# 1110 further matmuls behind the last instruction of TensorE in a fused attention and MLP kernel

## The chip, the cores and the metric

The kernel runs on one core of a Trainium2 chip. The metric is the device time of one execution in microseconds (us). Each engine of the core takes its own instructions in order: TensorE (PE, whose weight loads the profile lists apart as PEld), VectorE (DVE), ScalarE (ACT), GpSimd (POOL) and SyncE (SP, which here only issues DMAs). They meet in semaphores. The program is over when all of them have met in a barrier behind their last instruction.

## The reference

Attention over a window of 32 positions plus 32 global positions for 8 batches and 8 heads, and then an MLP with a GELU over the rows that it gives. Cut to what is computed:

```python
s_g = scale * np.matmul(q_g, k_all.transpose(0, 1, 3, 2))
out_g = np.matmul(sm(s_g), v_all)
mask = np.abs(pos[:, None] - pos[None, :]) <= window
s_ll = np.where(mask, scale * np.matmul(q_l, k_l.transpose(0, 1, 3, 2)), -1000000000.0)
s_l = np.concatenate([scale * np.matmul(q_l, k_g.transpose(0, 1, 3, 2)), s_ll], axis=-1)
out_l = np.matmul(sm(s_l), np.concatenate([v_g, v_l], axis=2))
...
h = x @ w_in                                          # 4352 x 512 by 512 x 2048
g = 0.5 * h * (1.0 + erf(h * inv_sqrt2))
return (g @ w_out).astype(np.float32)                 # 4352 x 2048 by 2048 x 512
```

## The kernel before

The 4352 rows are worked in 17 chunks of 256: sixteen of a batch and a half of its sequence, and one, called "g", of the global rows. For each chunk the attention of four pairs of heads yields x, and then the MLP runs over 16 slices f of 128 of the 2048 columns. For a slice, `ml_hc` makes h by products with four blocks of 128 rows of `w_in` (twelve matmuls of 256 columns), and `ml_o` adds to the two accumulators acc0 and acc1 (six matmuls of 512 columns). Every operand is split into a high and a low part of type float32r (x into `xh` and `xl`, GELU's output into `gh` and `gl`, the weights into `wh` and `wl`), and a product is taken as three: high by high, low by high and high by low. That is why the matmuls come in threes, lines 711 to 713 for h and 746 to 748 for acc:

```python
nc.tensor.matmul(out=h, lhsT=hi, rhs=xh, start=..., stop=False, skip_group_check=True)
nc.tensor.matmul(out=h, lhsT=hi, rhs=xl, start=False, stop=False, skip_group_check=True)
nc.tensor.matmul(out=h, lhsT=lo, rhs=xh, start=False, stop=..., skip_group_check=True)
```

Here `lhsT` is the stationary operand, 128 by 128, which a weight load brings into the array ahead of each matmul, and `rhs` is the moving one, whose 256 or 512 columns stream through. For h the weights are stationary and x moves; for acc the columns of g are stationary and the weights move.

A planner at the end of `attn_mlp` (a list of steps with needs, durations and due times) fixes the order, and the loop `for t, i, x in order` writes the steps out. It ties each instruction to the one before it on the same engine, through the table `last`, so that each engine's order is the planned one.

After the first chunks all 32 tiles of weights stay in SBUF to the end: `wh[n]` in halves of tiles of 1024 columns and `wl_[n]` in tiles of 512. PSUM holds eight banks of 512 columns; two of them, of the pool `ps_h` with the tag "h", take h in turn.

At the end of the program there is only the MLP of the chunk "g": TensorE alternates between twelve matmuls for h and six for acc, ScalarE and GpSimd prepare `gh` and `gl` beside it, and then `ml_e` copies the accumulators out (tile `ob`, line 134) and `ml_w` writes them to DRAM (line 761).

Of the kernel before, what the change touches and what calls it, by code (L numbers as in the profile page):

```python
# [8 lines left out]
F32 = mybir.dt.float32  # L9
# [75 lines left out]
def attn_mlp(ctx, tc, q_l, k_l, v_l, q_g, k_g, v_g, w_in, w_out, out):  # L85
# [1002 lines left out]
    for t, i, x in order:  # L1088
# [14 lines left out]
            taker[kind] = ins[seen].name, ins[seen].engine  # L1103
        seen = len(ins)


# [1 line left out]
_INS = ['q_l', 'k_l', 'v_l', 'q_g', 'k_g', 'v_g', 'moe_w_in', 'moe_w_out']  # L1108
# [26 lines left out]
```

## Time and profile before

| | us |
|---|---|
| median of 2 runs | 1043.26 |
| lowest, highest | 1042.47, 1044.06 |
| the profiled execution | 1045.66 |
| its span, first to last instruction | 1043.8 |
| TensorE busy in it | 1006.6 (96%) |
| granted TensorE clock, mean | 0.998 of full speed |

A row of the timeline has the start in us from the span's start, the duration, engine, line, operation and the tiles, written one first. Durations of matmuls overlap, because they are pipelined: how long one takes on TensorE is the distance from its start to that of the next, called its step below. Rounded to 0.01 us in the rows, it is read over many of them.

### The profile page before, as it was taken

The page shows a single profiled execution, that of the slowest core. Times are in us where ns is not written, and L with a number is a line of the kernel's source. Part 1 is how long each engine was busy: PE and PEld are TensorE (multiplying, and loading weights), DVE is VectorE, ACT ScalarE, POOL GpSimd, SP SyncE. Part 2 cuts the span into 40 slices and gives each one's busy share as a digit, 9 for nine tenths or more (in the row PEclk, how much of TensorE's full clock was granted, in tenths as well). Part 3 has the DMA queues.
Part 4 walks back from the last instruction along what each step waited for, and adds up shares of the span by engine and source line. Part 5 has one row for each costly group of instructions (what it writes and reads, how often), then busy time and mean ns, then how long its engine had stood idle before and what let it go on. Part 6 is the DMA issues. An engine that isn't in the chain of part 4 may idle for free.

```text
span 1043.8 us, 21420 instructions
## 1 busy us (share of the span) xinstructions
PE 1006.6 (96%) x7000; PEld 894.8 (86%) x7000; DVE 684.9 (66%) x2089; ACT 677.0 (65%) x1617; POOL 379.7 (36%) x427
## 2 busy tenths in 40 slices
PE   3889999999998999999999999999999999999998
PEld 2666689989888989898999989998999989999997
DVE  2878978667676877777775777677776777572000
ACT  2868887667567866677675766677575766674232
POOL 2111576243332533343442524334343525233121
PEclk9999999999999999999999999999999999999999
DMA  6877232223221233223322232313322332101000
GB/s 165 239 207 260 51 72 54 49 45 77 57 59 36 38 77 66 63 39 60 79 43 55 55 82 53 65 31 61 82 39 57 62 71 58 48 14 56 1 21 21
DMA packets 277983, 72.29 MB, mean 69 GB/s; under 512 B 263152, under 2 KB 271344, under 8 KB 277872
## 3 DMA queue, kind: packets, MB, share of 16 engines
q1 hardware_dynamic: 271792, 68.57, 28.7%
q10 hardware_dynamic: 6080, 2.36, 0.9%
q8 instruction: 55, 0.90, 0.4%
q14 instruction: 56, 0.46, 0.1%
HBM read 61.41 MB, written 9.44 MB: 68 GB/s over the span
## 4 chain that ended last, share of the span: by engine, by line
PE 75%; ACT 7%; SPq 6%; DMA 5%; DVE 4%; issue 2%; POOL 1%; ACTq 0%; DVEq 0%; POOLq 0%
PE h L711 10%; PE acc L746 9%; PE h L712 9%; PE h L713 9%; PE acc L748 9%; PE acc L747 9%; PE o L519 5%; PE s L408 4%; PE acc L738 2%; PE t L482 2%; ACT a_t L281 2%; PE h L707 2%; PE go L652 2%; ACT L281 1%; DMA raws<-in_q_l_dram 1%
## 5 line engine op out<-in xcount | busy, mean ns | idle before, releaser
L141 POOL TENSOR_TENSOR gl<-gf,gh 128x512 fp32r<-128x512 f32 x127 | 167.8, 1321 | 400.4 <-ACT gh L134 280.1
L711 PE MATMUL h<-xh,wh 128*128 128x256 f32 x1024 | 296.6, 290 | 1.4 <-ACT gf L281 1.4
L712 PE MATMUL h<-xl,wh 128*128 128x256 f32 x1024 | 286.1, 279 | 0.0
L713 PE MATMUL h<-xh,wl 128*128 128x256 f32 x1024 | 285.6, 279 | 0.0
L746 PE MATMUL acc<-wh,gh 128*128 128x512 f32 x512 | 204.9, 400 | 0.0
L711 PEld LDWEIGHTS h<-xh,wh 128*128 128x128 f32 x1024 | 192.7, 188 | 10.2 <-ACT gf L281 1.8
L748 PE MATMUL acc<-wl,gh 128*128 128x512 f32 x512 | 200.4, 391 | 0.0
L747 PE MATMUL acc<-wh,gl 128*128 128x512 f32 x512 | 200.2, 391 | 0.0
L712 PEld LDWEIGHTS h<-xl,wh 128*128 128x128 f32 x1024 | 193.0, 188 | 5.7 <-issue 0.7
L713 PEld LDWEIGHTS h<-xh,wl 128*128 128x128 f32 x1024 | 193.9, 189 | 0.0
L281 ACT ACTIVATE gf<-h 128x512 f32<-128x512 f32 x136 | 81.2, 598 | 69.4 <-POOL gl L141 34.9
L281 ACT ACTIVATE a_t<-a_t,sm 128x192 f32<-128x192 f32 (+1 forms) x256 | 116.8, 458 | 1.9 <-DVE sm L433 1.1
L748 PEld LDWEIGHTS acc<-wl,gh 128*128 128x128 f32 x512 | 96.1, 188 | 21.1
L427 DVE CUSTOM_DVE_ANT_0 a_t<-s,mask 128x192 f32<-128x192 f32 (+1 forms) x256 | 80.4, 368 | 44.0 <-PE s L408 43.8
L134 ACT ACTIVATE gh<-gf 128x512 fp32r<-128x512 f32 x95 | 60.0, 632 | 75.7 <-PE acc L748 74.7
L746 PEld LDWEIGHTS acc<-wh,gh 128*128 128x128 f32 x512 | 96.3, 188 | 12.2
L747 PEld LDWEIGHTS acc<-wh,gl 128*128 128x128 f32 x512 | 96.4, 188 | 11.2
L134 ACT ACTIVATE at<-t 128x512 fp32r<-128x512 f32 (+1 forms) x112 | 59.5, 542 | 48.2 <-PE t L483 21.2
L502 DVE TENSOR_TENSOR at<-t,at 128x512 fp32r<-128x512 f32 (+1 forms) x112 | 67.5, 617 | 34.6 <-ACT at L134 33.9
L141 POOL TENSOR_TENSOR vs<-vr,vs 128x512 fp32r<-128x512 f32 x56 | 74.6, 1332 | 41.8 <-DVE vs L136 19.9
L281 ACT ACT_TABLE_LOAD x69 | 88.5, 1283 | 1.2
L550 DVE TENSOR_TENSOR xs<-o,xs 64x256 f32<-64x256 f32 x112 | 46.1, 412 | 49.0 <-ACT xs L545 47.9
(132 smaller groups left out, 1736.1 us busy)
## 6 DMA issues: line engine op xcount, KB each, us to landing
wraw<-in_moe_w_out_dram SPq DMA_DIRECT2D x16, 512.0 KB, 7.8
raws<-in_v_l_dram SPq DMA_DIRECT2D x64, 128.0 KB, 2.5
out_dram<-ob SPq DMA_DIRECT2D x32, 256.0 KB, 2.2
raws<-in_k_l_dram SPq DMA_DIRECT2D x224, 36.0 KB, 1.9
vr<-in_v_l_dram SPq DMA_DIRECT2D x113, 64.0 KB, 2.1
wraw<-in_moe_w_in_dram SPq DMA_DIRECT2D x14, 512.0 KB, 7.6
raws<-in_q_l_dram SPq DMA_DIRECT2D x224, 32.0 KB, 1.8
raws<-in_v_g_dram SPq DMA_DIRECT2D x128, 16.0 KB, 1.9
```

The lines of the kernel that those rows point to most:

```text
L134: nc.scalar.activation(out=out, in_=in_, func=AF.Copy)
L141: (nc.vector if e == "v" else nc.gpsimd).tensor_sub(**kw)
L281: nc.scalar.activation(func=func, **kw)
L427: nc.vector.tensor_tensor_reduce(out=a_t[:, j, aoff[half][i]:aoff[half][i] + w], in0=s[:, c:c + w], in1=masks[half][i], scale=1.0, scalar= ...
L502: nc.vector.tensor_sub(out=at[:, 1], in0=st.pop((u, "t", j))[:, :n * P].rearrange("p (n q) -> p n q", q=P), in1=at.bitcast(F32)[:, 0])
L519: nc.tensor.matmul(out=o[:, :, qsl], lhsT=l.rearrange("p s e -> p (s e)"), rhs=r, start=(n == 0), stop=(n == 3), skip_group_check=True)
L711: nc.tensor.matmul(out=h, lhsT=hi, rhs=xh, start=(c == 0 and not (key == (0, 0) and f < HQ and f % 2)), stop=False, skip_group_check=True)
L712: nc.tensor.matmul(out=h, lhsT=hi, rhs=xl, start=False, stop=False, skip_group_check=True)
L713: nc.tensor.matmul(out=h, lhsT=lo, rhs=xh, start=False, stop=(c == NCC - 1), skip_group_check=True)
L746: nc.tensor.matmul(out=acc[t], lhsT=gh[:, f % 2, tsl], rhs=hi, start=(f == 0), stop=False)
L747: nc.tensor.matmul(out=acc[t], lhsT=gl[:, f % 2, tsl], rhs=hi, start=False, stop=False)
L748: nc.tensor.matmul(out=acc[t], lhsT=gh[:, f % 2, tsl], rhs=lo, start=False, stop=(f == NF - 1))
```

## The change

Behind the loop that writes out the plan, 1110 matmuls are appended whose results nothing reads. They read weights that lie in SBUF and write to the two banks of the tag "h". No step of the plan is changed, and no other engine gets an instruction.

- `mo()` stands for one acc step: six matmuls of 512 columns, three into each of two banks.
- `h(w, x)` stands for one h step: twelve matmuls of 256 columns into one bank, with the stationary operand from column w and the moving one from column x of their tiles.
- `both(w, x)` is twice a `mo()` and an `h(w, x)`, so 36 matmuls; it is called 28 times: 8 times with w = 0, 8 times with w = 64 and 12 times with other w. That is 336 matmuls of 512 columns and 672 of 256.
- The short runs repeat one matmul: six runs of ten with 256 columns, then four and three runs of six with 512 columns, so 60 and 42.

Together these are 378 of 512 columns and 732 of 256. In bytes, the places are these. Before, and with d = 0 in the new code, the moving operand of an h starts 192 bytes behind the stationary one, modulo 256; with d = 4, 8 or 12 columns it starts 208, 224 or 240 behind, and no longer at a multiple of 64. That holds for 348 of the 732 (288 in `h` and the 60 in runs). The moving and stationary operands of `mo` differ by 0 modulo 256, as they do in an acc before. In the runs of 512 columns 36 of 42 have the stationary operand at no multiple of 64 bytes.

```diff
+    def after_all(e0):
+        ins = nc.cur_bb.bb.instructions
+        for y in ins[e0:]:
+            if y.engine in last:
+                behind(y, last[y.engine])
+            last[y.engine] = y.name
+
+    code = iter([a + b for a in "abcdefghijkmnpqrstuvwxyz" for b in "abcdefghijkmnpqrstuvwxyz"])
+
+    def bank(n):
+        return n, ps_h.tile([P, 512], F32, name="z" + next(code), tag="h")
+
+    def mm(t, st_, mv):
+        n = mv.shape[-1]
+        nc.tensor.matmul(out=t[:, 0:n], lhsT=st_, rhs=mv, start=True, stop=True, skip_group_check=True)
+
+    e0 = len(nc.cur_bb.bb.instructions)
+    H = [wh[n] for n in range(2 * NF)]
+    LO = [wl_[n] for n in range(2 * NF)]
...
+    T1, T2, T3, T4, T5, T6 = H[2], H[6], H[10], H[14], LO[1], LO[9]
+
+    def run(a, b, n=8, w=256, A=None, B=None):
+        _, t = bank(0)
+        for _ in range(n):
+            mm(t, T5[:, b:b + P], T1[:, a:a + w])
+
+    def mo(lo=0):
+        t = [bank(0)[1] for _ in range(2)]
+        for i in range(2):
+            for m, g in ((T1, 64), (T1, 192), (T2, 64)):
+                mm(t[i], T5[:, g + 128 * i:g + 128 * i + P], m[:, 0:512])
+
+    def h(w, x):
+        _, t = bank(0)
+        for c in range(4):
+            for m, g in ((T3, T4), (T6, T4), (T3, LO[17])):
+                mm(t, g[:, w:w + P], m[:, x:x + 256])
+
+    def both(w, x):
+        for _ in range(2):
+            mo()
+            h(w, x)
+
+    for a in (48, 112):
+        for d in (0, 4, 8, 12):
+            both(0, a + d)
+    for a in (48, 112):
+        for d in (0, 4, 8, 12):
+            both(64, (a + d + 64) % 128)
+    for w in (16, 32, 48, 80, 96, 112):
+        for a in (48, 112):
+            both(w, (a + w) % 128)
+    for d in (4, 8, 12):
+        for a in (48, 112):
+            run(a + d, 0, 10)
+    for d in (0, 4, 8, 12):
+        run(0, 64 + d, 6, 512)
+    for d in (4, 8, 12):
+        run(0, d, 6, 512)
+    after_all(e0)
```

TensorE's last instructions before, in order, with the accumulators as `acc_13651` and `acc_13652`; "waits" names the engine whose semaphore a row waits for:

```order
L746 MATMUL acc_13651<-wh,gh 128x512 [waits Activation_49]
L747 MATMUL acc_13651<-wh,gl 128x512 [waits DVE_49]
L748 MATMUL acc_13651<-wl,gh 128x512
L746 MATMUL acc_13651<-wh,gh 128x512
L747 MATMUL acc_13651<-wh,gl 128x512
L748 MATMUL acc_13651<-wl,gh 128x512
L746 MATMUL acc_13652<-wh,gh 128x512
L747 MATMUL acc_13652<-wh,gl 128x512
L748 MATMUL acc_13652<-wl,gh 128x512
L746 MATMUL acc_13652<-wh,gh 128x512
L747 MATMUL acc_13652<-wh,gl 128x512
L748 MATMUL acc_13652<-wl,gh 128x512
L1130 UNCONDITIONAL_BRANCH
```

The branch ends TensorE's part. In the changed program it comes 1110 matmuls later; this is a stretch in the middle of them on the same engine, where zay and zba and zbb are banks of a `mo()` and zaz is that of an `h()`:

```order
L1120 MATMUL zay<-wh,wl 128x512 [waits PE_49]
L1120 MATMUL zay<-wh,wl 128x512 x2
L1120 MATMUL zaz<-wh 128x256 [waits PE_49]
L1120 MATMUL zaz<-wl,wh 128x256
L1120 MATMUL zaz<-wh,wl 128x256
...
L1120 MATMUL zba<-wh,wl 128x512 [waits PE_49]
L1120 MATMUL zba<-wh,wl 128x512 x2
L1120 MATMUL zbb<-wh,wl 128x512 [waits PE_49]
L1120 MATMUL zbb<-wh,wl 128x512 x2
```

What is new beside the matmuls is that each group's first row waits for TensorE's own semaphore: for the end of the group before the last, which wrote the same bank.

More of the change, by code (lines that the diff above doesn't have):

```diff
@@ L1104, in attn_mlp @@
         seen = len(ins)
+    def after_all(e0):
[13 more added lines that the diff above has]
+    LO = [wl_[n] for n in range(2 * NF)]
+    key = "g"
+    X = [st["xh", key, c] for c in range(NCC)]
+    Y = [st["xl", key, c] for c in range(NCC)]
+    G = st[key, "gh", NF // 2 - 1].rearrange("p a b -> p (a b)")
+    T1, T2, T3, T4, T5, T6 = H[2], H[6], H[10], H[14], LO[1], LO[9]
[34 more added lines that the diff above has]
+    after_all(e0)
 _INS = ['q_l', 'k_l', 'v_l', 'q_g', 'k_g', 'v_g', 'moe_w_in', 'moe_w_out']
```

## The prediction

> **What bounds the kernel now.** I read the page first, for the busiest engine and the clock, then a table of windows over the end of the program, since all of the change stands there, and then the timeline of TensorE in those windows.
>
> ```profile
> span 1043.8 us, 21420 instructions
> ...
> PE 1006.6 (96%) x7000; PEld 894.8 (86%) x7000; DVE 684.9 (66%) x2089; ACT 677.0 (65%) x1617; POOL 379.7 (36%) x427
> ...
> PE 75%; ACT 7%; SPq 6%; DMA 5%; DVE 4%; issue 2%; POOL 1%; ACTq 0%; DVEq 0%; POOLq 0%
> ```
>
> TensorE is busy for 96% of the span and holds 75% of the chain that ended last. The windows of the end have length, and then busy time and count of each engine, the granted clock, the DMA share and GB/s:
>
> ```profile
> core 0: us, PE busy (x) PEld busy (x) DVE busy (x) ACT busy (x) POOL busy (x), PEclk, DMA share, GB/s
> 1003.00:1010.00 7.00, 7.00 (x49) 6.46 (x48) 0.00 (x0) 1.23 (x2) 1.84 (x2) 1.00 0.00 0
> ...
> 1031.00:1038.00 7.00, 7.00 (x39) 6.03 (x38) 0.69 (x1) 1.23 (x2) 0.00 (x0) 1.00 0.00 0
> 1038.00:1044.00 6.00, 1.49 (x7) 0.91 (x5) 0.00 (x0) 1.20 (x2) 0.00 (x0) 0.90 0.33 87
> ```
>
> Over the last 36 us TensorE does not pause, at the full clock, and the other engines do little. Only the last 4.3 us are without it: its last matmul begins at 1039.10 and lasts 0.39, and then ScalarE copies the accumulator out and DMAs write it.
>
> ```profile
> 1038.79 2.73 SPq L761 DMA_DIRECT2D out_dram<-ob  x6
> ...
> 1039.10 0.39 PE L748 MATMUL acc<-wl,gh 128*128 128x512 f32 x1
> 1039.52 0.60 ACT L134 ACTIVATE ob<-acc 128x512 f32<-128x512 f32 x1 [0.76 <-PE acc L748]
> 1040.15 0.87 ACTq L761 DMA_DIRECT2D out_dram<-ob  x2
> ```
>
> Issuing ends at 1041.52; what remains to 1043.8 is landing and the closing barrier.
>
> **What one matmul costs there.** Every appended `both` is twice an acc step and an h step, and the end of the kernel is just that alternation. The first rows of the steps around one such pair, and of a pair seven further on:
>
> ```profile
> 1010.34 0.39 PE L746 MATMUL acc<-wh,gh 128*128 128x512 f32 x1
> ...
> 1011.70 0.28 PE L711 MATMUL h<-xh,wh 128*128 128x256 f32 x1
> ...
> 1013.11 0.39 PE L746 MATMUL acc<-wh,gh 128*128 128x512 f32 x1
> ...
> 1029.75 0.39 PE L746 MATMUL acc<-wh,gh 128*128 128x512 f32 x1
> ```
>
> From 1010.34 to 1029.75 there are seven pairs in 19.41 us, 2.773 us for a pair. Inside the first, six of 512 columns take 1011.70 - 1010.34 = 1.36 us, 0.2267 us each, and twelve of 256 take 1.41 us, 0.1176 each. The durations in the rows, 0.39 and 0.28, would count the pipeline's depth with each matmul, so I do not use them.
>
> **The change, step by step.** It removes nothing and moves nothing: the 5828 rows ahead of TensorE's branch keep their order and so do those of the other four engines. What it adds is one queue of work on TensorE behind everything else:
>
> - 56 pairs at 2.773 us: 155.3 us.
> - 60 matmuls of 256 columns in runs at 0.1176 us: 7.1 us.
> - 42 of 512 columns in runs at 0.2267 us: 9.5 us.
>
> The sum is 171.9 us. All of it lies on the path that sets the end, except what runs beside the tail that TensorE idles through today. The first added matmul needs no data of that tail: the weights have been in SBUF since the first chunks, and its bank was free long before. So it starts one step behind the last acc row, at 1039.10 + 0.23 = 1039.33, and the last one ends at 1039.33 + 171.9 + 0.16 = 1211.4, where 0.16 is the 0.39 of its own row less the step of 0.23. Copying out and writing the accumulators are hidden under the block, because they are over at 1043.8 at the latest. Behind TensorE's end there remain the last semaphore wait and the barrier. No row shows them alone; they are a part of the 2.3 us between 1041.52 and 1043.8, and part of that is landing. I take 1.0 us, with 0.5 and 2.3 as the ends. The span becomes 1212.4, 168.6 us more than before. The profiled execution took 1045.66 for its span of 1043.8, and would take 1214.3; it lies 2.4 above the median of the runs, against which the sum gives 1043.26 + 168.6 = 1211.9 us.
>
> **The places of the operands.** The 512-column groups and 384 of the 256-column matmuls keep the distance between moving and stationary operand that acc and h have in the trace, so their steps should be the same. Even there the step is not one number. These rows are the first of an h block and the row behind it, and then the first rows of two successive acc groups of three:
>
> ```profile
> 483.08 0.28 PE L711 MATMUL h<-xh,wh 128*128 128x256 f32 x1
> ...
> 484.44 0.39 PE L746 MATMUL acc<-wh,gh 128*128 128x512 f32 x1
> ```
>
> ```profile
> 513.98 0.39 PE L746 MATMUL acc<-wh,gh 128*128 128x512 f32 x1
> ...
> 514.68 0.39 PE L746 MATMUL acc<-wh,gh 128*128 128x512 f32 x1
> ```
>
> Twelve h matmuls in 1.36 us are 0.1133 each, and three acc matmuls in 0.70 are 0.233 each. With the faster h throughout, the sum falls by 732 x 0.0043 = 3.1 us; with the slower acc throughout it grows by 378 x 0.0066 = 2.5 us. I take the values of the end of the program, which is what the block continues without a break: from 1010.34 to 1029.75 no pair falls out of the 2.77.
>
> For the 348 matmuls whose moving operand starts off a multiple of 64 bytes, and the 36 with such a stationary operand, no row exists. Below, the nearest is the shortest step in the trace, that of transposes of 128 columns, where a weight load follows a weight load:
>
> ```profile
> 635.53 0.38 PE L482 MATMUL t<-ident,a_t 128*128 128x128 f32 x2
> 635.74 0.27 PE L483 MATMUL t<-ident,ge 128*128 128x128 f32 x1
> 635.85 0.27 PE L485 MATMUL t<-ident,ge 128*128 128x128 f32 x1
> ```
>
> Three steps in 0.32 us are 0.107, half as many columns in almost the time: the weight load sets it. That floor would save 348 x 0.0106 = 3.7 us. Above, the nearest is the step of a matmul with twice the columns, 0.2267, as if each shifted column were read twice: 348 x 0.109 = 38 us. A shift by 16 to 48 bytes out of the 1024 that one row of the operand spans is far nearer to no shift than to doubled reading, so I take the step of the unshifted.
>
> **The waits.** Each of the 168 groups in `both`, and each run, begins with a wait for the end of the group before the last. In 111 cases only three matmuls of 512 columns stand between. Where TensorE really waits in the trace, it starts again soon after the release (ScalarE's row, then the weight load that waited for it):
>
> ```profile
> 279.35 0.60 ACT L281 ACTIVATE gf<-h 128x512 f32<-128x512 f32 x1 [0.91 <-POOL gl L141]
> ...
> 280.00 0.19 PEld L711 LDWEIGHTS h<-xh,wh 128*128 128x128 f32 x1 [0.44 <-ACT gf L281]
> ```
>
> The copy ends at 279.95 and the load starts at 280.00, 0.05 later. In the block, the awaited matmul of 512 columns ends 0.39 after its start, and the waiting load would start when the third of the three begins, which is 3 x 0.227 = 0.68 after it: 0.29 us are left, for a release of 0.05. Behind a 256-column group it is 0.1176 + 2 x 0.227 - 0.28 = 0.29 as well. So I cost the waits at nothing; their cover is the group between. Waits that are fulfilled in time cost nothing in the trace either: the acc row at 1029.75, as every second one there, waits for ScalarE, and the seven pairs up to it still take 2.77 us each. If the cover were gone, what is behind the wait on TensorE is the block alone, and nobody else waits for it.
>
> **Rivals.** First, the waits do show. A matmul whose weight load has lost its lead costs about this much:
>
> ```profile
> 637.56 0.27 PE L483 MATMUL t<-ident,ge 128*128 128x128 f32 x1
> 637.59 0.36 PE L711 MATMUL h<-xh,wh 128*128 128x256 f32 x1
> 637.79 0.28 PE L712 MATMUL h<-xl,wh 128*128 128x256 f32 x1
> ```
>
> Here the step is 0.20 instead of 0.1176, 0.08 more. In 111 groups that is 9 us, and the time 1221. It would need a release of more than 0.29 us; against it stands the 0.05.
>
> Second, the shifted operands are read at up to double cost: up to 1250 us. Nothing in the trace speaks for it; nothing excludes it, as no such row exists.
>
> Third, the block runs at the floor of streaming, because the excess over it in the acc and h rows comes from two operands that get in each other's way and the new tiles lie elsewhere. With the transposes' 0.107 for 256 columns and twice that for 512 the block is 732 x 0.107 + 378 x 0.214 = 159 us, and the time 1199. Against it: the distances that acc and h have are kept for two thirds of the block. [...]
>
> Fourth, on the other side, no change: nothing reads the tiles zaa to zhn, and if the compiler drops matmuls with unread results, the program is the old one and takes 1043. It would also be 1043 if the block fitted under the 4.3 us that TensorE idles at the end, but that is reached below 20 matmuls, not at 1110. No row of the trace has an unread result, so this rests on the program as built, in which all 1110 stand.
>
> Fifth, the clock falls to a half in the block: 2 x 171.9, and 1384 us. The windows show 1.00 under a TensorE without pauses, which the block only prolongs.
>
> **How the numbers follow.** That the block runs at the steps of the kernel's end, with places that move it by a few us: 85%, 1212 us. Waits that show 5%, doubled reading or a good part of it 4%, the floor 2%, dropped 2%, clock 2%. The range is the first case with its bounds: below, 1212 - 3.1 - 3.7 = 1205; above, 1212 + 2.5 for the slower acc, 1.3 for a longer closing and some 3 for a tenth of the doubled reading, 1219. It leaves 15% out. Slower by over 2% (about what a measurement of this kernel can tell from no change) are all cases but the dropped block: 97%; within 2% is 2%, faster 1% for what I have not seen.
>
> **What would show it.** In the changed profile the rows up to 1039.5 stay as they are. The z rows follow at steps of 0.227 and 0.1176 with no idle time between groups, ending near 1211.4, with a clock of 1.00. Steps of 0.20 at the first row of a group would be the waits; steps that change with d from one `both` to the next would be the places; an end of TensorE's rows at 1039.5 would be the dropped block.

## The result and the profile after

The changed kernel takes 1213.93 us in the median of two runs (1212.53 and 1215.33), against 1043.26 before; the ratio is 1.1636, with a 95% interval from 1.1567 to 1.1705. The forecast was 1212, from 1205 to 1219. Timed once more in five rounds (below), it took 1212.88 beside 1042.93, a ratio of 1.1623 with an interval from 1.1608 to 1.1639.

The first lines of the page after, for TensorE and the other engines, and its shares of the chain that ended last:

```profile
span 1210.7 us, 23641 instructions
...
PE 1183.0 (98%) x8110; PEld 1054.8 (87%) x8110; DVE 683.7 (56%) x2089; ACT 676.6 (56%) x1617; POOL 379.5 (31%) x427
...
PE 83%; DVE 4%; ACT 3%; SPq 3%; DMA 2%; issue 1%; POOL 0%; DVEq 0%; ACTq 0%
```

TensorE has 1110 rows more, 8110 against 7000, and the other engines have the counts that they had. The block of added rows by windows (length, busy time and count of each engine, granted clock, DMA share, GB/s): two unshifted pairs and the mo behind them; from the first shifted h on, six pairs' worth up to the next unshifted h; from there to the end of the pairs; the runs of 256 columns; the runs of 512.

```profile
core 0: us, PE busy (x) PEld busy (x) DVE busy (x) ACT busy (x) POOL busy (x), PEclk, DMA share, GB/s
1036.43:1043.34 6.91, 6.91 (x43) 6.21 (x42) 0.00 (x0) 0.60 (x1) 0.00 (x0) 1.00 0.30 78
1043.34:1060.17 16.83, 16.83 (x109) 15.27 (x108) 0.00 (x0) 0.00 (x0) 0.00 (x0) 1.00 0.00 1
1060.17:1192.83 132.66, 132.66 (x859) 120.83 (x858) 0.00 (x0) 0.00 (x0) 0.00 (x0) 1.00 0.00 1
1192.83:1199.92 7.09, 7.09 (x62) 7.09 (x61) 0.00 (x0) 0.00 (x0) 0.00 (x0) 1.00 0.01 2
1199.92:1209.69 9.77, 9.77 (x44) 7.72 (x42) 0.00 (x0) 0.00 (x0) 0.00 (x0) 1.00 0.00 0
sum 173.26, PE 173.26 PEld 157.12 DVE 0.00 ACT 0.60 POOL 0.00; mean PE 34.65 PEld 31.42 DVE 0.00 ACT 0.12 POOL 0.00
```

There is no idle time and no lower clock, and the one ScalarE row of the old tail, with its DMAs (the 0.30 and 78 GB/s), lies in the first window, beside the block. All of the block is 173.26 us by steps, and the forecast had 171.9. Its beginning and end in the timeline, where rows of one bank are merged:

```profile
1036.21 0.39 PE L748 MATMUL acc<-wl,gh 128*128 128x512 f32 x1
...
1036.43 0.84 PE L1120 MATMUL zaa<-wh,wl 128*128 128x512 f32 x3
1037.11 0.84 PE L1120 MATMUL zab<-wh,wl 128*128 128x512 f32 x3
1037.79 0.28 PE L1120 MATMUL zac<-wh 128*128 128x256 f32 x1
...
1039.21 0.84 PE L1120 MATMUL zad<-wh,wl 128*128 128x512 f32 x3
```

```profile
1208.76 1.10 PE L1120 MATMUL zhn<-wh,wl 128*128 128x512 f32 x4
```

The block begins one step behind the last acc row, 0.22 after it, and the first pair takes 1039.21 - 1036.43 = 2.78 us, as the acc and h rows did. The last row ends at 1208.76 + 1.10 = 1209.86, 0.88 before the end of the span, which is 1210.74 in the trace before rounding.

### The profile page after: what moved, and what is told of

The parts are those of the page before. It is cut to its first block, busy times and chain, and to the rows that moved or that the text cites. A ratio compares the mean times of both kernels' runs of the same rounds, so it can differ in the third digit from the quotient of the medians.

```text
span 1210.7 us, 23641 instructions
## 1 busy us (share of the span) xinstructions
PE 1183.0 (98%) x8110; PEld 1054.8 (87%) x8110; DVE 683.7 (56%) x2089; ACT 676.6 (56%) x1617; POOL 379.5 (31%) x427
## 3 DMA queue, kind: packets, MB, share of 16 engines
q8 instruction: 64, 1.05, 0.4%
## 4 chain that ended last, share of the span: by engine, by line
PE 83%; DVE 4%; ACT 3%; SPq 3%; DMA 2%; issue 1%; POOL 0%; DVEq 0%; ACTq 0%
PE h L711 9%; PE h L712 8%; PE h L713 8%; PE acc L746 8%; PE acc L748 8%; PE acc L747 8%; PE o L519 4%; PE s L408 3%; PE h L707 2%; PE acc L738 2%; PE t L482 2%; PE go L652 1%; ACT a_t L281 1%; PE sg L565 1%; PE t L483 1%
```

## The experiments

Each kernel is the changed one with the edit shown; "rows" is the time from the start of the first added matmul to the start of the last, read from the trace. In the changed kernel it is 173.03 us. A mean step that has no row beside it is taken from the starts of all added matmuls of its kind.

**The waits taken away.** One bank, taken once, instead of two in turn.

```diff
+    one = ps_h.tile([P, 512], F32, name="z" + next(code), tag="h")
+
     def bank(n):
-        return n, ps_h.tile([P, 512], F32, name="z" + next(code), tag="h")
+        return n, one
```

> All 1110 added matmuls write to one bank taken once, so that the 181 waits at the heads of groups go (one is left) and nothing else changes. The forecast's theory, waits in time cost nothing: the added rows take 173.0 us from first to last start, as with the waits, within 0.3. The rival, that the waits show: up to 111 x 0.08 = 9 us less.

```profile
1036.42 1.07 PE L1122 MATMUL zaa<-wh,wl 128*128 128x512 f32 x4
```

```profile
1208.75 1.10 PE L1122 MATMUL zaa<-wh,wl 128*128 128x512 f32 x4
```

These are the lines with its first and last added matmuls; the second holds the last four. Their distance is 1208.75 - 1036.42 = 172.33 us, and in the changed kernel 1208.76 - 1036.43 = 172.33. Up to the start of the last matmul the rows take 173.03, and each step is the same in the two traces to 0.002 us; the time is 1212.52. So the 180 waits that are gone cost nothing that can be seen; the rival is out.

**All places aligned.**

```diff
-        for d in (0, 4, 8, 12):
+        for d in (0, 0, 0, 0):
...
-    for w in (16, 32, 48, 80, 96, 112):
+    for w in (0, 64, 0, 64, 0, 64):
...
-    for d in (4, 8, 12):
+    for d in (0, 0, 0):
```

> Same counts, but every shift d is 0 and every w is 0 or 64, so that all operands start at multiples of 64 bytes and h keeps the distance of 192 bytes throughout. If the steps of the changed kernel above 0.2267 and 0.1176 come from the shifted places, all steps fall to these and the added rows take 171.7 us, 1.3 less than 173.0. If the acc-like groups are slow of themselves, they stay at 0.2298 and the rows at 173.

One window over its block, from the first added row to one step behind the last:

```profile
1034.82:1206.72 171.90, 171.90 (x1111) 156.96 (x1109) 0.00 (x0) 0.60 (x1) 0.00 (x0) 1.00 0.02 4
```

The rows take 171.67 us; all 377 steps of 512 columns have a mean of 0.2267 and the 732 of 256 columns 0.1178. With the last step the block is 171.90, the sum of the forecast. So what the changed kernel has above it, 1.36 us, comes from the places: the shifts and the other columns w, which this edit takes away together.

**One pair only.**

```diff
-    for a in (48, 112):
...
-        run(0, d, 6, 512)
+    mo()
+    h(0, 48)
     after_all(e0)
```

> Only one mo and one h are added, 18 matmuls. The forecast's theory: they take 2.77 us and end about 2.9 us after the last acc row has ended, beside the copy and the writing of the last rows, so the time is that of before within 1 us. The rival, that any work on TensorE behind the last acc adds its own length: 2.8 us more.

Its DMAs, its last acc row, ScalarE's copy and the last added row:

```profile
1036.23 2.73 SPq L761 DMA_DIRECT2D out_dram<-ob  x6
...
1036.54 0.39 PE L748 MATMUL acc<-wl,gh 128*128 128x512 f32 x1
...
1036.97 0.60 ACT L134 ACTIVATE ob<-acc 128x512 f32<-128x512 f32 x1 [0.76 <-PE acc L748]
...
1039.42 0.28 PE L1120 MATMUL zac<-wh,wl 128*128 128x256 f32 x1
```

TensorE ends at 1039.70, 2.77 us after the end of its last acc row, and the span is 1041.2, 4.3 behind that row, as before. The medians are 1043.87 and, before, 1042.87 us. The ratio over ten runs is 1.0003, from 0.9988 to 1.0019, which is 1.3 us less to 2.0 us more: the rival's 2.8 us lies outside, and the tail hides the block.

**Starts off 16 bytes.** The shifts are 1, 2 and 3 columns.

```diff
-        for d in (0, 4, 8, 12):
+        for d in (0, 1, 2, 3):
...
-    for d in (4, 8, 12):
+    for d in (1, 2, 3):
```

> The shifts are 1, 2 and 3 columns instead of 4, 8 and 12, so that 348 moving and 36 stationary operands start off a multiple of 16 bytes. If a start off such a multiple costs one access more per operand, the steps grow by a few ns at most and the rows take 172 to 174.5 us. If it makes each column be read twice, 348 x 0.109 = 38 us more.

The rows take 173.16 us and the time is 1213.74. The mean step of 256 columns, over 116 rows each, is 0.1205 for a start 4 bytes off, 0.1203 for 8 and 0.1173 for 12, against 0.1180 for the 384 unshifted. No mean step comes near the 0.2267 of doubled reading. Whether a start off a multiple of 16 bytes costs anything of itself is neither shown nor excluded: the starts 4 and 8 bytes off have 2 to 3 ns more and those 12 off have none, but the three shifts always come in the same order and also change the distance to the stationary operand. In the changed kernel the same three places in the order, at multiples of 16 bytes, have 0.1187, 0.1184 and 0.1174, so about 2 ns at most are left for it.

**Other distances, all at multiples of 64 bytes.**

```diff
-    for a in (48, 112):
-        for d in (0, 4, 8, 12):
+    for a in (0, 64):
+        for d in (0, 16, 32, 48):
             both(0, a + d)
...
-    for w in (16, 32, 48, 80, 96, 112):
-        for a in (48, 112):
+    for w in (0, 64, 0, 64, 0, 64):
+        for a in (0, 64):
             both(w, (a + w) % 128)
```

The same is done with w = 64 and with the runs.

> In the h groups and runs the moving operand starts 0, 64, 128 or 192 bytes behind the stationary one modulo 256, always at a multiple of 64; before, it was 192 in every h. If the step of 256 columns depends on this distance, the four values show four steps; the rows of 256 columns at distance 0 in the kernel before (line 519) have 0.113 to 0.120. Then the added rows stay within 3 us of 173. If the distance does not matter, all are at 0.1176.

The rows take 173.91 us. The last 24 pairs have the distance 0, and the first rows of two of them, ten apart, show their rhythm:

```profile
1138.68 0.86 PE L1120 MATMUL zen<-wh,wl 128*128 128x512 f32 x3
```

```profile
1166.88 0.86 PE L1120 MATMUL zfu<-wh,wl 128*128 128x512 f32 x3
```

That is 28.20 us for ten, 2.820 a pair against 2.773 for the distance 192. In these pairs an h takes 1.432 us instead of 1.413, 1.6 ns more a step, and a mo, whose own operands are as they were, 1.388 instead of 1.360, 4.7 ns more a step. So the distance counts; its larger part shows in the neighbouring mo, and whether the distance within h or that to mo does it was not separated. The mean steps of 256 columns are 0.1193, 0.1181, 0.1191 and 0.1160 for 0, 64, 128 and 192 bytes, but they are no price of the distance alone: 192 has 0.1178 throughout in the aligned kernel, and here each stretch of it begins behind another distance, with an h of 1.376 us.

**Long stretches.**

```diff
+    for i in range(16):
+        mo()
+    for i in range(16):
+        h(0, 48)
+    run(52, 0, 10)
+    for i in range(16):
+        mo()
+    h(0, 48)
+    for i in range(16):
+        mo()
+    for i in range(8):
+        h(0, 52)
+    for i in range(8):
+        h(0, 48)
+    for i in range(8):
+        mo()
```

> Long stretches in place of the alternation: 96 matmuls of mo, 192 of h, a shifted run of 10, 96 of mo, one h of 12, 96 of mo, 96 of h shifted by 4 columns, 96 of h unshifted, 48 of mo; 336 of 512 columns and 406 of 256. If a step depends on the places of its own operands alone, all mo stand at 0.2267 and the two unshifted h stretches at 0.1176, in all about 124 us. If the shifted run leaves something behind that lasts, the second stretch of mo stands at 0.231 to 0.233 over all its 96 matmuls, 0.5 us more.

The windows are: mo, h unshifted, mo behind the shifted run, mo behind one h, h shifted, h unshifted behind it.

```profile
1034.40:1056.16 21.76, 21.76 (x98) 18.02 (x96) 0.00 (x0) 0.60 (x1) 0.00 (x0) 1.00 0.10 25
1056.16:1078.77 22.61, 22.61 (x193) 22.61 (x192) 0.00 (x0) 0.00 (x0) 0.00 (x0) 1.00 0.01 1
1079.96:1101.74 21.78, 21.78 (x99) 18.02 (x97) 0.00 (x0) 0.00 (x0) 0.00 (x0) 1.00 0.00 0
1103.15:1124.91 21.76, 21.76 (x98) 18.03 (x97) 0.00 (x0) 0.00 (x0) 0.00 (x0) 1.00 0.00 0
1124.91:1136.35 11.44, 11.44 (x97) 11.44 (x96) 0.00 (x0) 0.00 (x0) 0.00 (x0) 1.00 0.01 1
1136.35:1147.23 10.88, 10.88 (x98) 10.88 (x97) 0.00 (x0) 0.00 (x0) 0.00 (x0) 1.00 0.01 2
```

(A window's count also has the rows that reach into it from outside.) Each stretch of 96 mo matmuls takes 21.76 us, 0.2267 each; behind the shifted run it takes 0.02 more, which are its first two steps, 0.237 and 0.235. So what the shift leaves behind does not last in mo, against the rival. In h it does last, but the other way: 192 unshifted matmuls take 22.61, 0.1178 each, and the 96 behind the shifted h take 10.88, 0.1133 each, to the end of the stretch, with the same operands. Both theories fail on this: the same matmul had two lasting steps here, 0.1178 behind mo and 0.1133 behind the shifted h. They are the two that the trace of before shows for h. How what ran before makes the choice was not shown.

**All places moved by 64 bytes.** The changed kernel shows 2.80 us a pair with w = 16, although h keeps its distance there and all its starts are multiples of 64 bytes; these are the first rows of two successive pairs of it:

```profile
1134.22 0.86 PE L1120 MATMUL zej<-wh,wl 128*128 128x512 f32 x3
...
1137.02 0.63 PE L1120 MATMUL zen<-wh,wl 128*128 128x512 f32 x2
```

What w = 16 changes is the distance from a mo to the h behind it and back. Not every such change costs: with w = 48 the pairs are back at 2.77, as these first rows of two successive ones show.

```profile
1151.02 0.84 PE L1120 MATMUL zfd<-wh,wl 128*128 128x512 f32 x3
...
1153.79 0.39 PE L1120 MATMUL zfg<-wh,wl 128*128 128x512 f32 x1
```

A move by 64 columns, 256 bytes, changes nothing lasting: w = 80 has the 2.800 of w = 16, and w = 112 the 2.773 of w = 48. In the next kernel mo moves along.

```diff
-    T1, T2, T3, T4, T5, T6 = H[2], H[6], H[10], H[14], LO[1], LO[9]
+    T1, T2, T3, T4, T5, T6 = wh["tile", 4][:, 16:528], wh["tile", 6][:, 16:528], H[10], H[14], LO[1], LO[9]
...
-            for m, g in ((T1, 64), (T1, 192), (T2, 64)):
+            for m, g in ((T1, 80), (T1, 208), (T2, 80)):
...
+    for i in range(28):
+        both(16, 64)
```

Here `wh["tile", n]` is the whole tile that `wh[n]` is a half of. One of mo's two moving operands lies in another tile than before, as the right half `wh[2]` has no room for the move; modulo 256 bytes it too is 64 further on.

> 28 times the same both, with every added operand 64 bytes further on: mo's moving and stationary operands by 16 columns, and h with w = 16 and x = 64. All distances between operands, also those from one group to the next, are those of w = 0, x = 48. If distances alone set the steps, each pair of mo and h takes 2.773 us from the first to the last, as in the kernel with aligned places, and the 56 pairs take 155.3 us. The rival, that the place itself counts: with w = 16, x = 64 and mo left where it was, the changed kernel shows 2.80 for a pair, and 56 of them would take 156.8.

```profile
1138.99 0.84 PE L1121 MATMUL zen<-wh,wl 128*128 128x512 f32 x3
```

```profile
1191.68 0.84 PE L1121 MATMUL zgx<-wh,wl 128*128 128x512 f32 x3
```

These rows are 19 pairs apart: 52.69 us, 2.773 a pair. The first two pairs have 2.768 and 2.788, all others 2.773. The rows take 155.20 us, with the last step 155.3. So the place as such does not count here: with h where it was at w = 16, moving mo along brings 2.800 back to 2.773. What counted in these pairs is where the operands of a group lie against those of the groups beside it.

**A shorter weight load.** 96 equal matmuls with a stationary operand of 64 columns, then 96 with one of 128.

```diff
+    def m64(t, st_, mv):
+        nc.tensor.matmul(out=t[0:64, 0:512], lhsT=st_, rhs=mv, start=True, stop=True, skip_group_check=True)
...
+    for i in range(16):
+        mo()
+    _, t = bank(0)
+    for i in range(96):
+        m64(t, T5[:, 64:128], T1[:, 0:512])
+    _, t = bank(0)
+    for i in range(96):
+        mm(t, T5[:, 64:192], T1[:, 0:512])
```

> 16 mo, then 96 matmuls of 512 columns with a stationary operand of only 64 columns, which write 64 partitions, then the same 96 with one of 128 columns. If the excess of the 512-column step over plain streaming comes from the weight load that runs beside the stream, the first 96 fall below 0.2267, towards the 0.2155 that plain float32 of 256 columns shows in the kernel before, and the last 96 go back. If it comes from the stream of float32r itself, both stand at 0.2267.

The windows are the mo, the short loads and the full ones; below are the loads' own durations, with busy us, mean ns and idle time before.

```profile
1034.71:1056.47 21.76, 21.76 (x98) 17.97 (x97) 0.00 (x0) 0.60 (x1) 0.00 (x0) 1.00 0.09 25
1056.47:1078.55 22.08, 22.08 (x98) 12.93 (x97) 0.00 (x0) 0.00 (x0) 0.00 (x0) 1.00 0.00 1
1078.55:1100.31 21.76, 21.76 (x97) 17.84 (x95) 0.00 (x0) 0.00 (x0) 0.00 (x0) 1.00 0.00 1
```

```profile
L1120 PEld LDWEIGHTS zbj<-wh,wl 128*128 128x128 f32 x96 | 18.0, 188 | 3.8
L1138 PEld LDWEIGHTS zbi<-wh,wl 128*64 128x64 f32 x96 | 12.9, 134 | 9.1
```

The 0.2155 of the expectation is read in the kernel before, which works its first chunk in plain float32:

```profile
120.82 0.59 PE L707 MATMUL h<-xf,wf 128*128 128x256 f32 x2
121.25 1.88 PE L738 MATMUL acc<-wf,gf 128*128 128x512 f32 x4
```

The two matmuls of the first line take 121.25 - 120.82 = 0.43 us, 0.215 each. In the experiment a load of half the columns takes 134 ns instead of 188, and the step of the matmul rises to 22.08 / 96 = 0.230. Both expectations miss. The length of the load is not what holds the 512-column step above 0.2155; what does stays open. That the short ones also write only 64 partitions was not separated from the load.

**The changed kernel again**, without an edit.

> The changed kernel once more, timed in five rounds beside the kernel before. In the profiles the added rows begin one step behind the last acc row, take 173.0 us from first to last start, 0.39 for the last and 0.9 for the closing, 174.3 together, where the kernel before has 4.5 behind the same point. The theory that steps alone make the time: 169.8 us between the two medians, within 1.5. The rival, that the added rows also change the part ahead of them: a difference outside of that.

1212.88 - 1042.93 = 169.95 us; the interval of the ratio makes it 167.7 to 170.9. That is 0.15 from the 169.8 that the steps give, so no change in the part ahead of the block is seen.

## Why the prediction was right, point by point

**The steps.** Read from the last 20 us of the old trace, 0.2267 and 0.1176 us, they hold where the places are kept: 0.2267 and 0.1178 in the aligned kernel, and a block of 171.90 us against 171.9 forecast. (Twelve steps in 1.41 us are 0.1175, not 0.1176; on 732 matmuls either is within some 0.2 us of what was measured.) Using durations instead, 0.39 and 0.28, would have given 352 us for the block.

**The places.** This term was set at nothing, with a few us to either side, and is 1.36 us: the changed kernel's 173.26 less 171.90. One step of the forecast was wrong, though it cost little: matmuls that keep the distance between their own two operands were to keep their step. Over all added rows the mean step of 256 columns is 0.1179, hardly more than in the aligned kernel, and that of 512 columns 0.2301, so 378 x 0.0034 = 1.3 us lie in the matmuls of 512. Of these, 1.05 us are in mo, whose own operands are unshifted, and 0.24 in the short runs, where the stationary one is. By place, 0.68 of the 1.36 us lie in the 16 calls of `both` with w = 0 and 64, 0.41 in the 12 with other w, where h keeps its own distance, and 0.27 in the short runs. A mo is slow behind an h that lies otherwise to it: in long stretches two or three steps (0.237 and 0.235 behind the shifted run), in the alternation up to five of its six. The range had room for this through another term, the slower acc of 0.233 throughout, 2.5 us. The upper end adds some 3 us for a tenth of the doubled reading; a tenth of its 38 us is 3.8, which makes the end 1220. That bound was not near: the mean step of a start off 16 bytes is at most 3 ns above the unshifted.

**The waits.** They were costed at nothing and cost nothing: 173.03 us with and without.

**The tail and the closing.** The copy and the writing are hidden under the block, as forecast, and one pair alone is hidden under them. The closing behind TensorE's last row was an estimate without a row of its own, 1.0 us between 0.5 and 2.3, and is 0.88; that it came so near is in part luck.

**Against the median.** The sum gave 168.6 us. From the profiles, 1.36 more for the places and 0.12 less for the closing make 169.8, and the five rounds show 169.95. The first two runs have 170.7 between the medians, and the two runs after lie 2.8 apart. That scatter is not in the block, which takes 173.03 us in each of the two profiles of the changed kernel. It lies ahead of it: the block's first row is at 1036.43 and 1037.19 in these two, and would have been at 1039.33 in that of before. The profiles of before and after part within the first 84 us. There the first matmul starts, behind its DMA, at 10.2 and 9.9 us, and a window of 3.4 us at half the clock begins at 66.6 and 60.7; what each of these makes of the difference was not taken apart.

**The rivals.** No wait shows, no mean step comes near doubled reading, no matmul is dropped (8110 rows), and the clock stays at 1.00. The floor of the third rival, 0.107 and 0.214 us, is not reached: no long stretch of the runs is below 0.1133 and 0.2263 us a step (the second is the mo of 1.358 us at w = 48 and 112). The 0.107 is the step of transposes of 128 columns, whose weight loads of 0.14 us start 0.11 apart (at 635.64 and 635.75 us of the trace of before); that the load sets this step, and that it is a floor for 256 columns, was the author's estimate from these rows, and no run shows it. Nor does a run show two operands that get in each other's way: with equal instructions a pair takes 2.773, 2.800 or 2.820 us in a lasting rhythm, depending on where the operands lie to each other, but what makes the difference stays open, and a shorter load did not help (0.230 us a step against 0.2267).

## What to carry to other kernels

Cost added work on a saturated engine by the distance between starts in a stretch that does the same work, never by the durations of its rows, and add it behind the point where the engine ends today, less what the tail hides: here that came out within 1%. Waits on an engine's own earlier work cost nothing here (173.03 us with them and without); by the prediction's estimate the work between them left 0.29 us for a release of 0.05. Where operands lie to each other in SBUF moved a group of float32r matmuls by up to 2.5% (a mo of 1.360 us to 1.394 in the changed kernel) and a pair by about 2% (2.773 us to 2.820), so keep an order of matmuls and their distances together when a stage is copied elsewhere.

## What the runs showed of the hardware that was not expected

- In one run, matmuls of 256 columns had two lasting steps with the same operands: 0.1178 us behind mo, over 192 in a row, and 0.1133 us behind a shifted h, over 96.
- Steps depended on where the operands of successive matmuls lie to each other, also from group to group: 2.773 us a pair with all distances kept and all operands moved by 64 bytes, 2.800 with h alone moved by 64 bytes, 2.773 again with h moved by 192, 2.820 with h's operands at the distance 0. A further move of h by 256 bytes left the last three as they were.
- Halving the stationary operand's columns (and with them the partitions written) shortened its load from 188 to 134 ns and lengthened the step of 512 columns from 0.2267 to 0.230; why was not shown.
